# A new order of the opening of an attention and maxout kernel, with some weight work moved to GpSimd

## The chip, the cores and the metric

The kernel runs on one core of a Trainium2 chip. The metric is the device time of one execution in microseconds; 809.75 us is the median of three runs of the kernel before (809.45 to 810.16). Engine names are those of the profile: PE (TensorE matmul), PEld (its weight loads), DVE (VectorE), ACT (ScalarE), POOL (GpSimd), SP (SyncE, which issues the DMAs).

## The reference

There are 4 batches of 12544 tokens with 128 channels, and 32 inducing rows. All is float32.

```
def mab(q, kv):                       # attention without projections
    s = (q @ kv.T) / sqrt(128)
    a = softmax(s, axis=-1)           # maximum taken away, sum + 1e-9
    return a @ kv
h   = mab(inducing, x)                # 32 rows attend over 12544 tokens, per batch
y   = mab(x, h)                       # 12544 tokens attend over the 32 rows
out = maximum(maximum(y @ w1, y @ w2), y @ w3) @ w_out    # 128 -> 768 -> 128
```

The weights come in as 64-bit floats. The kernel reads them as pairs of 32-bit words and makes a float32 out of each pair on the chip.

## The kernel before, in words

**Tiling.** The 98 tiles of 128 tokens of a batch form seven groups: group 0 has 2 tiles, groups 1 to 6 have 16 each. Groups are handled in joint sets (1 with 0, 2 with 3, 4, 5 with 6), which share one running maximum.

**Staging.** The main part is a long run of slots, one per 512 tokens and 128 hidden columns, which is bound by PE: two products of the first layer, a maximum, a split of the result into a high and a low part, three products of the second layer. It needs `us`, the weights already multiplied with `h`. So before the first slot the whole first attention of batch 0 must be done, and the weights be converted. This opening is the head (`head`, L514): a list of steps in text (`HEAD`, L46), each of which issues the instructions of one step. The order of the text is the order on each engine, since every engine runs its own instructions in the order in which they were issued; a step that waits holds up all that stands behind it on its engine. No planner changes the order.

**The steps that the text below speaks of.** After the colon stands the group, the weight (0 is w2, 1 is w_out, 2 is w1, 3 is w3) or the part.

- `T:g.k`, `c:g.k`, `C:g.k`: four transposes of x on PE, and their copy to SBUF by ACT (`c`) or DVE (`C`).
- `S:g` scores (PE), `M:g` maximum (DVE), `D:g` a column of it (ACT), `G:g` and `L:g` the maximum of the joint set (PE, then DVE, L329), `K:g` its copy for the other member (POOL, L348), `E:g` the exponential (ACT, L336), `R:g` a transpose (DVE, L355), `U:g` the weighted sum of x (PE, L370), `H:g` its copy.
- For each weight: `n` the size of the high word (ACT, L187), `r` a scaling of the low word (DVE, L192), `m` a maximum (DVE, L195), `i` a shift (DVE, L199), `v` an integer addition (POOL, L203), `d` the sign put in (DVE, L207), all 128x768. `e:k.part.parts` is the difference of weight k and w2 (DVE, L219).
- `woh` and `wol`: w_out rounded (ACT, L560), and what the rounding left (POOL, L561).
- `least`, `wts`, `maskp`, `lw`, `tot`, `y`, `rec`, `hT`: the seven groups are combined into `h`, divided by the total, and transposed. `maskp` spreads the group weights on POOL (L622); `lw` (L641) sums the totals on DVE.
- `parts` and `p:0.*`, `p:2.*`: scores of the first tokens against `h`, and their softmax in nine steps (mostly DVE, L769 to L793). `turn` transposes the result for PE; `s:0` is the first product of the main part (L848).
- `up:k`, `hi:k`, `lo*:k`: the products of `h` and the weight differences (PE, L671), their high part (ACT, L676), their low part (L686). `mw` multiplies w2 and w_out (PE).

**Loads.** All first loads are issued by SP in one row (`first_loads`, L150, by `LOADS`): x0, w2, x1 in four pieces, x2, x3, w1, x4, x5, w3, x6 in four pieces, w_out. All DMAs share the same engines and come in about in this order.

Of the kernel before, what the change touches and what calls it, by code (L numbers as in the profile page):

```python
# [26 lines left out]
def kernel(ctx, tc, x, xt, ind_t, w1, w2, w3, w_out, out):  # L27
    nc = tc.nc
    B, N, C = x.shape
    M = ind_t.shape[1]  # L30
# [15 lines left out]
    HEAD = """  # L46
        n:0 r:0 F:17 T:1.1 T:1.0 m:0 i:0 C:1.0 c:1.1 T:1.2 c:1.2 T:1.3 C:1.3 T:0.0 S:1 c:0.0 S:0 M:1 M:0 D:1 D:0 v:0
        d:0 T:2.2 C:2.2 T:2.3 c:2.3 T:2.0 c:2.0 G:1 L:1 K:0 T:2.1 C:2.1 E:1 T:3.3 E:0 c:3.3 T:3.2 T:3.0 c:3.0 T:3.1
        n:2 C:3.2 R:1 r:2 m:2 R:0 i:2 c:3.1 S:2 M:2 U:1 S:3 M:3 U:0 HV:1 T:4.1 C:4.1 v:2 D:2 D:3 T:4.2 c:4.2 G:2 L:2
        E:2 d:2 R:2 e:2.0.1 T:4.3 T:4.0 c:4.0 c:4.3 E:3 R:3 T:5.2 c:5.2 n:3 S:4 M:4 D:4 r:3 m:3 i:3 K:3 v:3 U:2  # L50
        T:5.0 c:5.0 T:5.1 c:5.1 G:4 L:4 E:4 T:5.3 C:5.3 T:6.0 C:6.0 T:6.2 c:6.2 T:6.1 c:6.1 R:4 T:6.3 c:6.3 S:5 d:3
        M:5 S:6 M:6 U:3 n:1 m:1 r:1 D:5 D:6 G:5 L:5 K:6 i:1 v:1 H:2 U:4 E:5 e:3.0.2 R:5 E:6 least R:6 H:4 w2T U:5
        U:6 wts lw maskp tot H:5 y:1 y:2 w2h d:1 woh wol y:4 y:5 rec hT parts:0 parts:2 e:3.1.2 p:0.0 p:0.1 p:0.2
        p:0.3 p:2.0 up:0 up:1 hi:0 hi:1 lop:1 p:0.4 p:0.5 p:2.1 p:0.6 p:0.7 up:2 hi:2 mw p:2.2 p:2.3 cw p:0.8 turn:0
        pca:0 turn:1 pca:1 lov:0 lov:2 p:2.4 s:0 up:3 hi:3 N:1 s:1 s:2 p:2.5 N:1 s:3 s:4 p:2.6 N:1 s:5 next p:2.7
        x:0 lov:3 s:6 p:2.8 q:0 q:1 x:1 q:2 q:3 q:4 q:5 q:6 q:7
    """
# [43 lines left out]
    def load_group(b, gi, pieces=1):
        g = groups[gi]
        if g["nt"] == GT:
            xg = xgs_free.pop(0) if xgs_free else xts_free.pop().rearrange("p (t c) -> p t c", c=C)
        else:
            xg = short_x
        n = g["nt"] // pieces
        for k in range(0, g["nt"], n):
            nc.sync.dma_start(out=xg[:, k : k + n, :], in_=xv[b, :, g["t0"] + k : g["t0"] + k + n, :])
# [72 lines left out]

    def weight_size(k):
        v = raws[k].rearrange("p (k two) -> p two k", two=2)
        words[k] = v[:, 0, :], v[:, 1, :]
        sized[k] = hp.tile([P, DF], F32, name="size", tag="size", bufs=2)
        nc.scalar.activation(out=sized[k], in_=words[k][1].bitcast(F32), func=AF.Abs)  # L187

    def weight_rest(k):
        rests[k] = hp.tile([P, DF], F32, name="rest", tag="rest", bufs=2)  # L190
        low = raws[k].rearrange("p (k two) -> p two k", two=2)[:, 0, :]
        nc.vector.tensor_scalar(out=rests[k], in0=low, scalar1=2.0**-51, scalar2=2.0, op0=ALU.mult, op1=ALU.add)  # L192

# [975 lines left out]
```

## Time and profile before

| | us |
|---|---|
| median of three runs | 809.75 |
| span of the profiled execution | 807.8 |
| PE busy, of the span | 799.0 (99%) |
| DVE busy | 647.2 (80%) |
| ACT busy | 714.4 (88%) |
| POOL busy | 656.7 (81%) |

The page gives no time of its own for the profiled execution beside its span. The median stands 1.95 us above the span; that is what lies around it (start and end of the launch). A difference in the span is carried to the median one to one.

A row of the timeline reads: start in us from the span's start, length in us, engine, line, operation, output <- input, partitions x elements, count, and in brackets the idle time before it with what ended it.

### The profile page before, as it was taken

To read this page: it belongs to the slowest core of one execution; us is meant where nothing else is said; L and a number is where in the kernel's file an instruction comes from. 1 tells how busy PE (TensorE), PEld (TensorE's weight loads), DVE (VectorE), ACT (ScalarE), POOL (GpSimd) and SP (SyncE) were. 2 spreads that over 40 slices of the span, in tenths; PEclk is the share of its full clock that TensorE was granted. 3 is DMA by queue.
4 is the path that set the end of the run, shared out by engine and by line. 5 is a ranking of instruction groups with operands and counts; after the bars stand their busy time and mean duration, and the time that the engine had idled before them with its cause. 6 is when DMAs were issued, how large, how long until landed. Compare 5 with 4: busy or idle time off the path is not lost.

```text
span 807.8 us, 15028 instructions
## 1 busy us (share of the span) xinstructions
PE 799.0 (99%) x4565; PEld 629.1 (78%) x4565; DVE 647.2 (80%) x1193; ACT 714.4 (88%) x1435; POOL 656.7 (81%) x637
## 2 busy tenths in 40 slices
PE   8999999999999999999999999999999999999998
PEld 6677778777787787787777877877778778777886
DVE  5988778779787797797976977978878878878874
ACT  4799889889898898898988988989899999999996
POOL 2379888888798898897887988979788879878886
PEclk9999999999999999999999999999999999999999
DMA  8526553442553434435463344334142222222221
GB/s 351 195 101 201 185 170 104 139 140 98 158 178 111 146 121 151 141 108 177 127 184 101 118 155 132 110 125 128 56 110 71 66 78 67 75 77 79 60 80 52
DMA packets 45408, 101.47 MB, mean 126 GB/s; under 512 B 9360, under 2 KB 15376, under 8 KB 40208
## 3 DMA queue, kind: packets, MB, share of 16 engines
q1 hardware_dynamic: 45184, 100.39, 39.8%
q8 instruction: 36, 0.59, 0.3%
q14 instruction: 44, 0.36, 0.1%
q10 hardware_dynamic: 144, 0.13, 0.0%
HBM read 48.12 MB, written 25.69 MB: 91 GB/s over the span
## 4 chain that ended last, share of the span: by engine, by line
PE 95%; DMA 2%; ACT 1%; DVE 0%; issue 0%; SPq 0%; DVEq 0%
PE acc L942 50%; PE pu L848 16%; PE pv L854 16%; PE aux L730 3%; PE acc L936 3%; DMA xg<-in_x_dram 2%; PE acc L488 2%; PE aux L391 2%; PE aux L297 0%; PE acc L370 0%; PE aux L692 0%; ACT ru L863 0%; PE pv L281 0%; PE pu L281 0%; ACT a L336 0%
## 5 line engine op out<-in xcount | busy, mean ns | idle before, releaser
L878 POOL TENSOR_TENSOR lo<-h,hi 128x512 fp32r<-128x512 f32 (+1 forms) x498 | 621.2, 1277 | 111.3 <-ACT hi L870 54.7
L886 DVE TENSOR_TENSOR h<-pv,ru 128x512 f32<-128x512 f32 (+1 forms) x512 | 342.6, 672 | 129.3 <-PE pv L854 104.6
L863 ACT ACTIVATE ru<-pu 128x512 f32<-128x512 f32 (+1 forms) x600 | 368.2, 614 | 66.2 <-PE pu L848 61.9
L870 ACT CAST hi<-h 128x512 fp32r<-128x512 f32 (+1 forms) x512 | 320.1, 625 | 1.1 <-PE acc L942 0.7
L942 PE MATMUL acc<-hi,wo_hi 128*128 128x512 f32 (+1 forms) x601 | 234.8, 391 | 0.0
L848 PE MATMUL pu<-pT,us 128*128 128x512 f32 (+1 forms) x600 | 232.0, 387 | 0.3 <-ACT ru L863 0.2
L854 PE MATMUL pv<-pT,us 128*128 128x512 f32 (+1 forms) x600 | 231.6, 386 | 0.0
L942 PE MATMUL acc<-hi,wo_lo 128*128 128x512 f32 (+1 forms) x601 | 231.4, 385 | 0.0
L942 PE MATMUL acc<-lo,wo_hi 128*128 128x512 f32 (+1 forms) x601 | 231.3, 385 | 0.0
L942 PEld LDWEIGHTS acc<-hi,wo_hi 128*128 128x128 f32 x601 | 112.8, 188 | 41.3 <-issue 19.7
L848 PEld LDWEIGHTS pu<-pT,us 128*128 128x128 f32 x600 | 112.6, 188 | 24.3 <-issue 0.8
L854 PEld LDWEIGHTS pv<-pT,us 128*128 128x128 f32 x600 | 112.6, 188 | 23.5 <-DVE h L886 0.3
L942 PEld LDWEIGHTS acc<-lo,wo_hi 128*128 128x128 f32 x601 | 112.8, 188 | 22.9
L942 PEld LDWEIGHTS acc<-hi,wo_lo 128*128 128x128 f32 x601 | 112.9, 188 | 21.7
L886 DVE TENSOR_TENSOR aux<-pv,ru 128x512 f32<-128x512 f32 x66 | 45.7, 693 | 9.8 <-PE pv L854 3.5
L889 DVE TENSOR_TENSOR lo<-aux,hi 128x512 fp32r<-128x512 f32 x66 | 45.3, 686 | 1.4 <-PE acc L942 0.8
L870 ACT CAST hi<-aux 128x512 fp32r<-128x512 f32 x66 | 41.7, 632 | 0.1
L954 ACT COPY shelf<-acc 128x512 f32<-128x512 f32 (+1 forms) x65 | 39.1, 602 | 0.0
L936 PE MATMUL acc<-pT,us 128*128 128x512 f32 (+1 forms) x100 | 38.8, 388 | 0.0
L432 POOL COPY mq<-mq 32x1 f32<-32x1 f32 (+2 forms) x108 | 20.4, 189 | 5.2
L730 PE MATMUL aux<-xT,hT 128*32 128x512 f32 x184 | 24.5, 605 | 0.0
L488 PEld LDWEIGHTS acc<-xg,aT 128*32 128x32 f32 x576 | 16.8, 110 | 8.5 <-issue 7.8
(186 smaller groups left out, 549.2 us busy)
## 6 DMA issues: line engine op xcount, KB each, us to landing
out_dram<-shelf SPq DMA_DIRECT2D x95, 256.0 KB, 2.0
xg<-in_x_dram SPq DMA_DIRECT2D x22, 1024.0 KB, 5.9
xT<-in_xt_dram SPq DMA_DIRECT2D x18, 1024.0 KB, 5.1
pT<-ph SPq DMA_DIRECT2D x184, 64.0 KB, 2.0
pT<-pl SPq DMA_DIRECT2D x184, 64.0 KB, 2.0
raw<-in_w_dram SPq DMA_DIRECT2D x3, 768.0 KB, 11.0
us<-uh SPq DMA_DIRECT2D x24, 52.0 KB, 3.2
us<-ul SPq DMA_DIRECT2D x24, 52.0 KB, 1.9
```

Of the source, the lines that this page charges most:

```text
L488: nc.tensor.matmul(out=st["h"][q * M : (q + 1) * M, :], lhsT=aT[:, t * M : (t + 1) * M], rhs=row, start=(t < NQ), stop=(t + NQ >= len(rows)),)
L730: nc.tensor.matmul(out=sp[q * M : (q + 1) * M, :w], lhsT=st["hT"][:, :M], rhs=xT[:, q * w : (q + 1) * w], start=True, stop=True)
L848: nc.tensor.matmul(out=pu[:, :w], lhsT=state[c.b]["us"][:, 2 * j * P : (2 * j + 1) * P], rhs=c.pT[:, :w], start=True, stop=True)
L854: nc.tensor.matmul(out=pv[:, : d.w], lhsT=state[d.b]["us"][:, (2 * j + 1) * P : (2 * j + 2) * P], rhs=d.pT[:, : d.w], start=True, stop=True,)
L863: nc.scalar.activation(out=ru[:, :w], in_=pu[:, :w], func=AF.Relu)
L870: nc.scalar.copy(out=hi[:, : c.w], in_=h[:, : c.w])
L878: nc.gpsimd.tensor_sub(**args)
L886: nc.vector.tensor_max(out=h[:, : d.w], in0=pv[:, : d.w], in1=relus.pop(s)[:, : d.w])
L889: nc.vector.tensor_sub(**low)
L936: nc.tensor.matmul(out=c.acc[:, :w], lhsT=us[:, 2 * DF :], rhs=c.pT[:, :w], start=(base == 0), stop=False)
L942: nc.tensor.matmul(out=c.acc[:, cs], lhsT=lhs[:, j, :], rhs=rhs[j][:, cs], start=(j < base and j == 0 and lhs is wo_hi and rhs is c.hh), s ...
L954: (nc.vector.tensor_copy if by_vector else nc.scalar.copy)(out=o[:, : c.w], in_=c.acc[:, : c.w])
```

## The change

It rewrites the list of steps of the head and the order of the loads. Of the loads, the first seven keep their order; after x3 comes w3 in place of w1, and w_out and w1 come last. It adds four kinds of steps that run on GpSimd: `rp` and `mp` (the scaling and the maximum of a weight, in place of DVE), `wohp` (the rounding of w_out, in place of ACT), and `ep` (which the kernel before already knew) is now used for all three differences, in place of DVE. The spreading of the group weights (`maskp`) goes the other way, from POOL to DVE (`mask`). A step `w` is defined and not used.

```diff
-    LOADS = (0, 7, 1, 2, 3, 9, 4, 5, 10, 6, 8)
+    LOADS = """
+        ind x0 w2 x1.0 x1.1 x1.2 x1.3 x2 x3 w3 x4 x5 x6.2 x6.3 x6.0 x6.1 wo w1
+    """
     HEAD = """
-        n:0 r:0 F:17 T:1.1 T:1.0 m:0 i:0 C:1.0 c:1.1 T:1.2 c:1.2 T:1.3 C:1.3 T:0.0 S:1 c:0.0 S:0 M:1 M:0 D:1 D:0 v:0
...
-        M:5 S:6 M:6 U:3 n:1 m:1 r:1 D:5 D:6 G:5 L:5 K:6 i:1 v:1 H:2 U:4 E:5 e:3.0.2 R:5 E:6 least R:6 H:4 w2T U:5
-        U:6 wts lw maskp tot H:5 y:1 y:2 w2h d:1 woh wol y:4 y:5 rec hT parts:0 parts:2 e:3.1.2 p:0.0 p:0.1 p:0.2
-        p:0.3 p:2.0 up:0 up:1 hi:0 hi:1 lop:1 p:0.4 p:0.5 p:2.1 p:0.6 p:0.7 up:2 hi:2 mw p:2.2 p:2.3 cw p:0.8 turn:0
...
+        F:17 T:0.0 c:0.0 T:1.1 C:1.1 T:1.2 T:1.0 C:1.0 T:1.3 c:1.2 C:1.3 S:0 n:0 S:1 M:1
+        M:0 D:1 D:0 T:2.1 T:2.3 C:2.3 mp:0 T:2.2 C:2.2 G:1 T:2.0 c:2.1 L:1 T:3.2 E:1 E:0 T:3.1 C:2.0 R:1 T:3.0 R:0 c:3.2
+        T:3.3 c:3.1 S:2 U:1 n:3 i:0 c:3.0 r:0 C:3.3 S:3 U:0 T:4.2 T:4.3 M:2 T:4.1 rp:3 m:3 M:3 c:4.2 i:3 T:4.0 C:4.3 D:2
+        D:3 G:2 T:5.2 L:2 c:4.1 c:4.0 E:2 E:3 T:5.3 v:0 d:0 T:5.1 K:0 S:4 HV:1 c:5.3 R:3 c:5.1 M:4 c:5.2 D:4 T:5.0 T:6.3
+        T:6.2 c:5.0 G:4 T:6.1 T:6.0 v:3 S:5 d:3 c:6.3 L:4 E:4 ep:3.1.2 C:6.2 C:6.1 c:6.0 R:2 n:1 n:2 R:4 S:6 U:2 rp:1
+        M:5 M:6 D:5 D:6 ep:3.0.2 r:2 m:2 U:3 G:5 L:5 H:2 U:4 i:2 E:5 mp:1 K:3 H:4 K:6 least R:5 i:1 E:6 wts R:6 w2T w2h
+        mask U:5 U:6 H:5 lw y:1 v:2 tot y:2 d:2 y:4 rec v:1 y:5 N:1 hT d:1 parts:0 p:0.0 ep:2.0.1 parts:2 wohp wol p:0.1
+        up:2 up:1 p:0.2 p:2.0 p:0.3 hi:2 p:0.4 p:0.5 up:0 p:0.6 mw p:2.1 hi:1 p:0.7 p:2.2 hi:0 lop:1 p:0.8 lov:0 p:2.3
+        turn:0 lov:2 turn:1 pca:0 p:2.4 cw pca:1 s:0 s:1 s:2 N:1 p:2.5 s:3 s:4 p:2.6 s:5 next x:0 p:2.7 s:6 up:3 q:0 q:1
+        hi:3 p:2.8 x:1 q:2 q:3 lov:3 q:4 N:1 q:5 q:6 q:7
...
+    def weight_rest(k, engine):
+        weight_words(k)
         rests[k] = hp.tile([P, DF], F32, name="rest", tag="rest", bufs=2)
-        low = raws[k].rearrange("p (k two) -> p two k", two=2)[:, 0, :]
-        nc.vector.tensor_scalar(out=rests[k], in0=low, scalar1=2.0**-51, scalar2=2.0, op0=ALU.mult, op1=ALU.add)
-
-    def weight_least(k):
-        nc.vector.tensor_scalar(out=sized[k], in0=sized[k], scalar1=LEAST, scalar2=None, op0=ALU.max)
+        engine.tensor_scalar(out=rests[k], in0=words[k][0], scalar1=2.0**-51, scalar2=2.0, op0=ALU.mult, op1=ALU.add)
+
+    def weight_least(k, engine):
+        engine.tensor_scalar(out=sized[k], in0=sized[k], scalar1=LEAST, scalar2=None, op0=ALU.max)
...
-        nc.sync.dma_start(out=iT, in_=ind_t)
+        first_loads()
         nc.scalar.mul(out=iT, in_=iT, mul=scale)
-        first_loads()
...
-            "r": weight_rest,
-            "m": weight_least,
+            "r": lambda k: weight_rest(k, vec),
+            "rp": lambda k: weight_rest(k, pool),
+            "m": lambda k: weight_least(k, vec),
+            "mp": lambda k: weight_least(k, pool),
...
-            "woh": lambda: nc.scalar.copy(out=wo_hi, in_=wo),
+            "woh": lambda: act.copy(out=wo_hi, in_=wo),
+            "wohp": lambda: pool.tensor_copy(out=wo_hi, in_=wo),
```

In the new list the instructions of DVE from the maximum of group 5 and 6 on are, in order: `L:5 i:2 least R:5 i:1 R:6 mask lw d:2 rec hT d:1 p:0.0`. Those of POOL are, from the first: `mp:0 rp:3 v:0 K:0 v:3 ep:3.1.2 rp:1 ep:3.0.2 mp:1 K:3 K:6 v:2 v:1 ep:2.0.1 wohp wol lop:1`. In the list before, DVE has `L:5 i:1 e:3.0.2 R:5 least R:6 lw d:1 rec hT e:3.1.2 p:0.0`, and POOL `v:0 K:0 v:2 K:3 v:3 K:6 v:1 maskp wol lop:1`.

## Rows read from the trace of the kernel before

**Rows 1.** The page, busy time of PE, and its chain by engine.
```profile
PE 799.0 (99%) x4565; PEld 629.1 (78%) x4565; DVE 647.2 (80%) x1193; ACT 714.4 (88%) x1435; POOL 656.7 (81%) x637
...
PE 95%; DMA 2%; ACT 1%; DVE 0%; issue 0%; SPq 0%; DVEq 0%
```

**Rows 2.** Stretches of the head: start:end, length, each engine's busy time, granted clock, DMA.
```profile
18.00:27.00 9.00, 8.43 (x104) 6.26 (x94) 8.77 (x18) 7.00 (x16) 3.43 (x3) 1.00 1.04 385
27.00:30.00 3.00, 3.00 (x40) 1.49 (x41) 2.79 (x5) 2.71 (x6) 1.06 (x1) 1.00 0.10 33
30.00:34.00 4.00, 3.61 (x94) 2.89 (x87) 4.00 (x10) 2.38 (x9) 2.22 (x2) 1.00 0.00 0
```

**Rows 3.** Timeline of PE: the last transposes, the scores, `up:0` and `s:0`.
```profile
27.34 0.60 PE L281 MATMUL pv<-shelf,xT 128*128 128x128 f32 x4
27.88 1.96 PE L297 MATMUL aux<-xT,shelf 128*32 128x512 f32 x16
...
38.17 1.13 PE L671 MATMUL acc<-shelf,hT 128*128 128x512 f32 x2
...
43.12 0.39 PE L848 MATMUL pu<-pT,us 128*128 128x256 f32 x1
```

**Rows 4.** Issues of the pieces of x6: first and last start, time to landing.
```profile
L109 SPq DMA_DIRECT2D xT<-in_x_dram x4: 328/328/328, 8.6 to 14.2; - x4
...
xT<-in_x_dram SPq DMA_DIRECT2D x1, 256.0 KB, 12.2
```

**Rows 5.** Timeline of POOL in the head.
```profile
14.32 0.18 POOL L348 COPY mneg<-mneg 128x1 f32<-128x1 f32 x1 [4.12 <-DVE mneg L329]
18.63 1.82 POOL L203 TENSOR_TENSOR rest<-rest,size 128x768 int32<-128x768 int32 x1 [4.13 <-DVE size L199]
20.78 0.85 POOL L348 COPY mneg<-mneg 128x1 f32<-128x1 f32 x1 [0.33 <-DVE mneg L329]
...
31.67 0.45 POOL L348 COPY mneg<-mneg 128x1 f32<-128x1 f32 x1 [3.61 <-DVE mneg L329]
32.22 2.02 POOL L203 TENSOR_TENSOR rest<-rest,size 128x768 int32<-128x768 int32 x1
...
37.16 1.90 POOL L561 TENSOR_TENSOR wo_lo<-xT,wo_hi 128x768 fp32r<-128x768 f32 x1 [2.40 <-ACT wo_hi L560]
```

**Rows 6.** Timeline of DVE in the head.
```profile
20.64 0.95 DVE L207 SCALAR_TENSOR_TENSOR dst<-raw,rest 128x768 uint32<-128x768 uint32 x1
...
22.26 0.92 DVE L219 TENSOR_TENSOR shelf<-dst,xT 128x768 f32<-128x768 f32 x1
...
29.91 0.69 DVE L307 TENSOR_REDUCE mq<-aux 128x1 f32<-128x512 f32 x1 [0.21 <-PE aux L297]
...
31.45 0.16 DVE L329 TENSOR_REDUCE mneg<-acc 128x1 f32<-128x8 f32 x1
31.53 0.55 DVE L199 TENSOR_SCALAR size<-size 128x768 uint32<-128x768 uint32 x1
...
32.46 0.70 DVE L355 STREAM_TRANSPOSE aT<-a 128x512 f32<-128x512 f32 x1
...
33.13 0.71 DVE L355 STREAM_TRANSPOSE aT<-a 128x512 f32<-128x512 f32 x1
33.76 0.50 DVE L641 TENSOR_TENSOR lw<-w,lst 128x7 f32<-128x7 f32 x1
34.30 0.16 DVE L643 TENSOR_REDUCE l<-lw 128x1 f32<-128x7 f32 x1
...
36.16 0.35 DVE L652 RECIPROCAL rec<-rec 128x32 f32<-128x32 f32 x1 [0.26 <-DVE rec L651]
36.62 0.29 DVE L657 TENSOR_TENSOR hT<-pu,rec 128x128 f32<-128x128 f32 x1
...
37.73 0.40 DVE L769 STREAM_TRANSPOSE pv<-pv 128x192 f32<-128x192 f32 x1 [0.35 <-PE pv L748]
```

**Rows 7.** POOL by groups, first two us: operations with one input or none; busy us, mean ns.
```profile
masks.py:199 POOL TENSOR_SCALAR_AFFINE_SELECT shelf<-shelf 128x128 f32<-128x128 f32 x1 | 0.3, 295 | 0.1
```

More of the change, by code (lines that the diff above doesn't have):

```diff
@@ L46 @@
     HEAD = """
-        n:0 r:0 F:17 T:1.1 T:1.0 m:0 i:0 C:1.0 c:1.1 T:1.2 c:1.2 T:1.3 C:1.3 T:0.0 S:1 c:0.0 S:0 M:1 M:0 D:1 D:0 v:0
[L48 to L51, printed above, removed]
-        M:5 S:6 M:6 U:3 n:1 m:1 r:1 D:5 D:6 G:5 L:5 K:6 i:1 v:1 H:2 U:4 E:5 e:3.0.2 R:5 E:6 least R:6 H:4 w2T U:5
-        U:6 wts lw maskp tot H:5 y:1 y:2 w2h d:1 woh wol y:4 y:5 rec hT parts:0 parts:2 e:3.1.2 p:0.0 p:0.1 p:0.2
-        p:0.3 p:2.0 up:0 up:1 hi:0 hi:1 lop:1 p:0.4 p:0.5 p:2.1 p:0.6 p:0.7 up:2 hi:2 mw p:2.2 p:2.3 cw p:0.8 turn:0
-        pca:0 turn:1 pca:1 lov:0 lov:2 p:2.4 s:0 up:3 hi:3 N:1 s:1 s:2 p:2.5 N:1 s:3 s:4 p:2.6 N:1 s:5 next p:2.7
-        x:0 lov:3 s:6 p:2.8 q:0 q:1 x:1 q:2 q:3 q:4 q:5 q:6 q:7
+        F:17 T:0.0 c:0.0 T:1.1 C:1.1 T:1.2 T:1.0 C:1.0 T:1.3 c:1.2 C:1.3 S:0 n:0 S:1 M:1
[8 more added lines that the diff above has]
+        hi:3 p:2.8 x:1 q:2 q:3 lov:3 q:4 N:1 q:5 q:6 q:7
     """
@@ L98, with space_for, load_tiles, load_group @@
     xv = x.rearrange("b (p t) c -> b p t c", t=NT)
[L101 to L109, printed above, removed]
+    def space_for(gi):
+        if groups[gi]["nt"] < GT:
+            return short_x
+        return xgs_free.pop(0) if xgs_free else xts_free.pop().rearrange("p (t c) -> p t c", c=C)
+    def load_tiles(b, gi, xg, a, z):
+        t0 = groups[gi]["t0"]
+        nc.sync.dma_start(out=xg[:, a:z, :], in_=xv[b, :, t0 + a : t0 + z, :])
+    def load_group(b, gi):
+        xg = space_for(gi)
+        load_tiles(b, gi, xg, 0, groups[gi]["nt"])
         return xg
@@ L144, in load_raw @@
         return r
-    srcs = [w2.bitcast(U32), w_out.bitcast(U32).rearrange("(j p) c -> p j c", p=P), w1.bitcast(U32), w3.bitcast(U32)]
+    srcs = {
+        "w2": (0, w2.bitcast(U32)),
+        "wo": (1, w_out.bitcast(U32).rearrange("(j p) c -> p j c", p=P)),
+        "w1": (2, w1.bitcast(U32)),
+        "w3": (3, w3.bitcast(U32)),
+    }
     raws = {}
-    FULLS = [gi for gi in LOADS if 0 < gi < NG]
+    SPARE_HOME = NG - 1
     def first_loads():
-        for what in LOADS:
-            if what < NG:
-                state[0]["xg"][what] = load_group(0, what, pieces=4 if what in (FULLS[0], FULLS[-1]) else 1)
-            else:
-                raws[what - NG] = load_raw(srcs[what - NG])
+        xgs = state[0]["xg"]
+        xgs.update({gi: space_for(gi) for gi in range(NG)})
+        for what in LOADS.split():
+            if what == "ind":
+                nc.sync.dma_start(out=iT, in_=ind_t)
+            elif what in srcs:
+                k, src = srcs[what]
+                raws[k] = load_raw(src)
+            else:
+                gi, piece = ([int(n) for n in what[1:].split(".")] + [None])[:2]
+                a, z = (0, groups[gi]["nt"]) if piece is None else (4 * piece, 4 * piece + 4)
+                load_tiles(0, gi, xgs[gi], a, z)
     ident = place(P)
@@ L181, with weight_words, weight_size @@
     words, sized, rests, floats = {}, {}, {}, {}
-    def weight_size(k):
+    def weight_words(k):
         v = raws[k].rearrange("p (k two) -> p two k", two=2)
         words[k] = v[:, 0, :], v[:, 1, :]
+    def weight_size(k):
+        weight_words(k)
         sized[k] = hp.tile([P, DF], F32, name="size", tag="size", bufs=2)
         nc.scalar.activation(out=sized[k], in_=words[k][1].bitcast(F32), func=AF.Abs)
-    def weight_rest(k):
+    def weight_rest(k, engine):
+        weight_words(k)
         rests[k] = hp.tile([P, DF], F32, name="rest", tag="rest", bufs=2)
-        low = raws[k].rearrange("p (k two) -> p two k", two=2)[:, 0, :]
-        nc.vector.tensor_scalar(out=rests[k], in0=low, scalar1=2.0**-51, scalar2=2.0, op0=ALU.mult, op1=ALU.add)
-    def weight_least(k):
-        nc.vector.tensor_scalar(out=sized[k], in0=sized[k], scalar1=LEAST, scalar2=None, op0=ALU.max)
+        engine.tensor_scalar(out=rests[k], in0=words[k][0], scalar1=2.0**-51, scalar2=2.0, op0=ALU.mult, op1=ALU.add)
+    def weight_least(k, engine):
+        engine.tensor_scalar(out=sized[k], in0=sized[k], scalar1=LEAST, scalar2=None, op0=ALU.max)
     def weight_shift(k):
@@ L199, in weight_shift, with weight_join @@
         nc.vector.tensor_scalar(out=bits, in0=bits, scalar1=3, scalar2=None, op0=ALU.logical_shift_left)
+    def weight_join(k):
+        whole = rests[k].bitcast(I32)
+        nc.gpsimd.scalar_tensor_tensor(
+            out=whole, in0=sized[k].bitcast(I32), scalar=8, in1=whole, op0=ALU.mult, op1=ALU.add
+        )
     def weight_whole(k):
@@ L360, in attend_sums @@
         st = state[b]
-        xg, aT = st["xg"].pop(gi), st["a"].pop(gi)
+        xg, aT = st["xg"][gi], st["a"].pop(gi)
         members = JOINT[LEADER[gi]]
-        if gi == FULLS[-1]:
+        if gi == SPARE_HOME:
             xts_free.append(xg.rearrange("p t c -> p (t c)"))
@@ L554, in head @@
             "n": weight_size,
-            "r": weight_rest,
-            "m": weight_least,
+            "r": lambda k: weight_rest(k, vec),
+            "rp": lambda k: weight_rest(k, pool),
+            "m": lambda k: weight_least(k, vec),
+            "mp": lambda k: weight_least(k, pool),
             "i": weight_shift,
+            "w": weight_join,
             "v": weight_whole,
             "d": weight_sign,
-            "woh": lambda: nc.scalar.copy(out=wo_hi, in_=wo),
+            "woh": lambda: act.copy(out=wo_hi, in_=wo),
+            "wohp": lambda: pool.tensor_copy(out=wo_hi, in_=wo),
             "wol": lambda: nc.gpsimd.tensor_sub(out=wo_lo, in0=wo, in1=wo_hi.bitcast(F32)),
@@ L665, in first_products @@
     def first_products(st, which, bank):
-        if which == 0:
+        if "us" not in st:
             st["us"] = bp.tile([P, UW], F32R, name="us", tag="us")
```

## The prediction

> **What bounds the kernel now.** I read the page first: PE is busy 99% of the span, and the chain of work that ended last lies on PE for 95% [rows 1]. Behind the head there is nothing to win for a change that touches the head alone; it moves the time by as much as it moves the first product of the main part, `s:0`, at 43.12 [rows 3]. The dense part then ends as much earlier or later. So the question is which wait ends last before `s:0`. For that I read, in this order, the stretches of the head, then the timelines of PE, POOL and DVE side by side.
>
> In the stretches the reader is to see that loads aren't the limit at the end. DMA works to the 27th us; the last piece of x6 was issued at 14.2 and landed 12.2 later, at 26.4 [rows 4], but its transposes came at 27.34 behind the ones before them, on a PE that was busy for 3.00 of 3 us [rows 2, 3]. Before that PE stood idle for 9.00 − 8.43 = 0.57 us in 18 to 27 [rows 2]. From 30 on DVE is the full engine (4.00 of 4) [rows 2], and the chain runs through it: `L:5` (31.45), the transposes `R:5` and `R:6`, the reciprocal, `hT` (36.62), then the softmax `p:0.0` (37.73), and from there 43.12 − 37.73 = 5.39 us to `s:0` [rows 3, 6].
>
> In POOL's rows the reader is to see one more thing. A copy of 128x1 took 0.18 us at 14.32, but 0.85 at 20.78, which ends at 21.63, just when DVE's sign step `d` (20.64 + 0.95 = 21.59) is done; and 0.45 at 31.67, ending at 32.12, when DVE's shift of 31.53 (+ 0.55 = 32.08) is done. The other way round, `lw`, seven columns, took 0.50 on DVE from 33.76, and ended at 34.26, with POOL's `v` (32.22 + 2.02 = 34.24) [rows 5, 6]. So POOL and DVE shut each other out, for a whole instruction, where DVE works from SBUF on two inputs (`d`, `lw`) or on one at double rate (the shift: 0.55 for 768 columns, against 0.92 for the two-input difference of 768 [rows 6]). Operations of DVE that read PSUM, and the transposes, ran beside `v` at their usual length: `R:5` 0.70 and `R:6` 0.71, both inside `v` [rows 5, 6].
>
> By the Trainium skill, SBUF — State Buffer, section "SBUF: two separate sides", the two engines share one pair of ports as an exclusive lock, held for the whole instruction, against DVE operations in a two-port mode or with two SBUF inputs; the trace agrees, with the 0.85, the 0.45 and the 0.50. What the trace of before does not show is the one case of a double-rate DVE operation that waits for POOL; by the page it would, and then the second case below falls away.
>
> **The change, part by part.**
>
> *Loads.* x6 comes about 2 us earlier, w1 takes w_out's place as the last. PE can win at most the 0.57 us that it stood idle; w1's conversion `n:2, r:2, m:2` simply stands where w_out's `n:1, r:1, m:1` stood. SP issues as many loads as before, in one row, and the later ones of batch 1 are not needed before the main part. I take 0 to −0.6.
>
> *Work taken from DVE.* Up to `L:5` it is four scalings and maxima and the difference of w1, 4 x 0.55 + 0.92 = 3.1 us. It does not come off the path there: `M:6` waited 0.21 for PE [rows 6], not for DVE. So 0.6, PE's idle time, is about the most by which `L:5` can come earlier.
>
> *Work given to POOL.* A one-input operation of 128x768 is not in the trace. From below, 128x128 took 0.295 and 128x1 0.18 [rows 5, 7], so 0.18 + 768/128 x 0.115 = 0.87; from above, a two-input one took 1.82 to 1.90 [rows 5]. I take 1.0, near the one-input row. It is not its length that I count, but whom it shuts out: `i:0`, `m:3`, `d:0` and `r:2` on DVE now fall due while POOL works on `rp:3`, `v:0`, `v:3` or the row `ep:3.1.2 rp:1 ep:3.0.2 mp:1`. A part of one instruction each, 0 to 1 us, partly in the shadow of other waits; I set it against the 0.6 and take `L:5` at 31.45 as before. Bounds: 30.85 without such waits, and 34.1 if the new operations take 1.9 (1.9 for the one in front of `r:2`, 0.8 more of `mp:1` in front of `v:2`).
>
> By the Trainium skill, GPSIMD Engine Reference, section "4.1 Engine selection", an operation with one input runs there at about line rate; with the 1.2 GHz of its section "1. Specifications" that is an estimate of 768/1.2 = 640 ns, which no row here shows; the sum would by it come to some 0.3 less.
>
> *The end of the head.* Here three POOL instructions of 1.8 to 1.9 us (`v:2`, `v:1`, `ep:2.0.1`) stand just where DVE has five two-input or double-rate ones (`i:1`, `mask`, `lw`, `d:2`, `d:1`), in front of the chain. From `L:5` at 31.45:
>
> - `i:2` 31.53 to 32.08, as the shift did before [rows 6]; `v:2` on POOL 32.13 to 33.95 (1.82 [rows 5]).
> - `R:5` 32.46 to 33.16, as before. `i:1` is due at 33.1 and waits for `v:2`, 0.85: 33.95 to 34.50. `R:6` stands behind it: 34.45 to 35.16, where it ended at 33.84 before (+1.3).
> - `v:1` needs `i:1`: 34.55 to 36.37. `mask` is due at 35.16 and waits 1.2 for `v:1`. Its length is between 0.29 (128x128) and 0.92 (128x768) [rows 6]; 0.38 in proportion: to 36.75. The group sums `y` and U:6 are in its shadow.
> - `lw` and its sum, 0.16 each (34.30 [rows 6]), to 37.1; `d:2` 0.95 to 38.05; `rec` is the reciprocal with the idle time in front of it, 0.35 + 0.26, and an addition as short as the 0.16 of 34.30, 0.8 in all: to 38.85, `hT` 0.3 to 39.2. It was 36.91 before: +2.3.
> - `ep:2.0.1` needs `d:2`: POOL 38.1 to 40.0 (1.90 as `wol`). `d:1`, new between `hT` and `p:0.0`, is due at 39.2, waits 0.8, and ends at 40.95. `p:0.0` then starts at 40.95, and not at 37.73: **+3.2**.
>
> Behind that the nine softmax steps are the same: 5.39 us to `s:0`. The `up` products can start when `ep` is done, at 40.0, and three of 1.13 at most (38.17 [rows 3]) end at 43.4, and `mw` behind them well before `s:0` is due at 46.3. `wohp` and `wol` on POOL (1.0 + 1.9 behind `d:1`, to 43.9) are done before `s:0`, and `wo_lo` is used behind it; ACT, through which the chain doesn't pass here, loses the rounding. Cost 0.
>
> Sum: 0 + 3.2 + 0; 807.8 becomes 811.0, and with the 1.95 us around the span, 809.75 becomes **812.9**. The bounds of this case: 812.3 with `L:5` at 30.85, 815.6 with it at 34.1.
>
> **The rivals.**
>
> 1. *Only two-input operations of DVE wait for POOL.* For it: `lw` is the only DVE instruction whose wait for POOL is seen whole. Against it: the copy of 0.45 behind the shift. `i:1` then doesn't wait (`v:1` starts at 33.95, ends 0.57 earlier), and `L:5` comes 0.6 earlier: 3.2 − 1.2 = +2.0, **811.7**.
> 2. *The engines don't get in each other's way here* (POOL's int32 and one-input operations leave room for DVE). Not slower: `hT` comes 0.2 earlier than before, since `R:6`, `mask` and `lw` follow at once; `d:1` (0.95) then fills the place of the half difference and of the 0.35 that `p:0.0` waited. **809.5**. Against it: the 0.50 of `lw`, behind this same `v`. It decides if `mask` starts within 0.1 of the end of `R:6`.
> 3. *DVE's queue sets the pace of the whole head* (8.77 of 9 us and 4.00 of 4 [rows 2]), and what is taken from it shows: of the 3.1 us, some 2, since not all of it falls due after 18 us. **807.7**. Against it: `M:6` waits for PE.
> 4. *The granted clock falls in the pauses of PE* that the waits make. It is 1.00 (2.4 GHz) in every stretch [rows 2]; at 1.2 GHz the three `up` products on the path behind `hT`, some 3 us, take 3 us more on top of the forecast: **816**. No row of before shows a fall.
>
> **How the numbers follow.** Forecast 55%, rival 1 15%, rival 2 15%, rival 3 10%, rival 4 5%. About 0.2%, 1.6 us, is what a measurement of this kernel can tell from no change. Slower by more: all of the forecast, most of rival 1 (0.09, its price being near the limit) and rival 4, 0.69; the same: 0.06 and 0.13 of rival 2, 0.19; faster: rival 3 and the rest of rival 2, 0.12. The range runs from 809.0 to 815.0; it leaves out rivals 3 and 4 and the far end of the forecast. The likeliest case's own range is 812.0 to 815.6.
>
> **What would show it.** `i:1` (128x768 shift on DVE) that ends with `v:2`, and lasts longer than 0.55 or starts late; `mask` that ends just behind `v:1`; `d:1` that ends about 0.95 behind `ep:2.0.1`; `hT` near 39 and `p:0.0` near 41, `s:0` near 46.3, and the same 5.4 us between them; `L:5` near 31.5; POOL's new operations near 1 us. I am wrong if `p:0.0` comes before 39, if `mask` runs inside `v:1`, or if `s:0` is late and the end is not.

## The result and the profile after

The changed kernel is slower: 814.16 us (median of 5 runs, 813.55 to 815.25) against 809.75 (5 runs beside it, 809.45 to 810.29). The ratio is 1.0055, with a 95% interval of 1.0042 to 1.0067. The same kernel in a second series gave 814.05, ratio 1.0056 (1.0043 to 1.0069). The forecast was 812.9, the range 809.0 to 815.0.

The profiled execution is the slowest of its five, with an own time of 815.25 and a span of 813.5; the other four have spans of 811.7 to 812.9. The page (engine: busy, share, instructions; TensorE's clock in slices of 20 us; the chain by engine):

```profile
PE 802.2 (99%) x4565; PEld 629.9 (77%) x4565; DVE 649.9 (80%) x1189; ACT 711.7 (87%) x1432; POOL 666.6 (82%) x644
...
PEclk9989999999999999999999999999999999999999
...
PE 95%; DMA 2%; DVE 1%; ACT 1%; issue 0%; SPq 0%; DVEq 0%; ACTq 0%
```

As before [rows 1], PE is busy 99% of the span and the chain lies on it. What is new on the page is the 8 in the third slice of PEclk: the granted clock was lower somewhere between 41 and 61 us; the stretches below show that the fall began at 39. The stretches of the head (columns as in [rows 2]: length, then PE, PEld, DVE, ACT, POOL, then the clock):

```profile
27.00:30.00 3.00, 3.00 (x62) 1.67 (x64) 1.23 (x3) 2.68 (x5) 3.00 (x4) 1.00 0.10 33
30.00:34.00 4.00, 2.48 (x66) 1.99 (x59) 3.83 (x9) 1.79 (x7) 2.40 (x4) 1.00 0.00 0
34.00:38.00 4.00, 2.64 (x69) 1.89 (x67) 4.00 (x5) 1.89 (x7) 3.21 (x2) 1.00 0.01 4
...
39.00:45.00 6.00, 5.99 (x33) 2.87 (x33) 5.65 (x14) 0.90 (x2) 4.44 (x3) 0.50 0.67 240
```

Two things stand in them. From 27 to 30 DVE does only 1.23 us of work, where it did 2.79 [rows 2]: it waits. And from 39 to 45 the clock is 0.50 (1.2 GHz of 2.4), after eight microseconds, 30 to 38, in which PE was busy 5.1 of 8. DVE's timeline (columns as in [rows 6]; line numbers have moved: L381 is `R`, L333 `M`, L355 `L`, L219 `i`, L233 `d`, L798 `p:0.0`) shows where the time went:

```profile
18.67 1.21 DVE L215 TENSOR_SCALAR size<-size 128x768 f32<-128x768 f32 x1
...
30.00 0.71 DVE L381 STREAM_TRANSPOSE aT<-a 128x512 f32<-128x512 f32 x1 [1.77 <-ACT size L207]
30.64 1.25 DVE L333 TENSOR_REDUCE mq<-aux 128x1 f32<-128x512 f32 x2
...
32.74 0.16 DVE L355 TENSOR_REDUCE mneg<-acc 128x1 f32<-128x8 f32 x1
32.85 0.56 DVE L219 TENSOR_SCALAR size<-size 128x768 uint32<-128x768 uint32 x1
...
34.38 1.44 DVE L219 TENSOR_SCALAR size<-size 128x768 uint32<-128x768 uint32 x1
35.74 0.70 DVE L381 STREAM_TRANSPOSE aT<-a 128x512 f32<-128x512 f32 x1
36.37 1.66 DVE L651 TENSOR_TENSOR mask<-shelf,w 128x224 f32<-128x224 f32 x1
37.95 0.15 DVE L670 TENSOR_TENSOR lw<-w,lst 128x7 f32<-128x7 f32 x1
...
39.79 0.29 DVE L686 TENSOR_TENSOR hT<-pu,rec 128x128 f32<-128x128 f32 x1
40.00 1.86 DVE L233 SCALAR_TENSOR_TENSOR xT<-raw,rest 128x768 uint32<-128x768 uint32 x1
41.78 0.39 DVE L798 STREAM_TRANSPOSE pv<-pv 128x192 f32<-128x192 f32 x1
```

and POOL's, beside it, whom these DVE instructions waited for (L215 is `mp`, L212 `rp`, L229 `v`, L245 `ep`, L589 `wohp`; in DVE's rows L215 is `m`, L212 `r`, L651 `mask`):

```profile
17.63 1.83 POOL L229 TENSOR_TENSOR rest<-rest,size 128x768 int32<-128x768 int32 x1 [0.96 <-DVE rest L212]
...
27.31 0.95 POOL L212 TENSOR_SCALAR rest<-raw 128x768 f32<-128x768 uint32 x1
...
29.19 2.14 POOL L215 TENSOR_SCALAR size<-size 128x768 f32<-128x768 f32 x1
...
33.57 1.84 POOL L229 TENSOR_TENSOR rest<-rest,size 128x768 int32<-128x768 int32 x1
35.96 1.81 POOL L229 TENSOR_TENSOR rest<-rest,size 128x768 int32<-128x768 int32 x1 [0.56 <-DVE size L219]
39.24 1.81 POOL L245 TENSOR_TENSOR shelf<-dst,xT 128x768 f32<-128x768 f32 x1 [1.46 <-DVE dst L233]
41.93 0.83 POOL L589 CAST wo_hi<-xT 128x768 fp32r<-128x768 f32 x1 [0.88 <-DVE xT L233]
```

PE's timeline, the last scores of the head and the sums `U:2` and `U:3` behind them, the first `up` product (L700), and `s:0` (L877), which answer to [rows 3]:

```profile
27.08 1.93 PE L323 MATMUL aux<-xT,shelf 128*32 128x512 f32 x16
28.82 1.93 PE L396 MATMUL acc<-xg,aT 128*32 128x128 f32 x64
...
42.22 2.07 PE L700 MATMUL pv<-shelf,hT 128*128 128x512 f32 x2
...
48.79 0.38 PE L877 MATMUL pu<-pT,us 128*128 128x256 f32 x1 [0.18 <-ACT pT L558]
```

Cut as the prediction cut it, against the rows of before [rows 3, 6]:

| | before | after | difference | forecast |
|---|---|---|---|---|
| to `L:5` | 31.45 | 32.74 | +1.29 | 0 |
| `L:5` to `p:0.0` | 6.28 | 9.04 | +2.76 | +3.2 |
| `p:0.0` to `s:0` | 5.39 | 7.01 | +1.62 | 0 |
| `s:0` | 43.12 | 48.79 | +5.67 | +3.2 |
| span | 807.8 | 813.5 | +5.7 | +3.2 |

So the span did move with `s:0`, one to one. The middle term came near the forecast; the first and the last were put at nothing and were not. The experiments were to say what made each of the three.

### The profile page after: what moved, and what is told of

The parts are those of the page before. It is cut to its first block, busy times and chain, and to the rows that moved or that the text cites. A ratio compares the mean times of both kernels' runs of the same rounds, so it can differ in the third digit from the quotient of the medians.

```text
span 813.5 us, 14942 instructions
## 1 busy us (share of the span) xinstructions
PE 802.2 (99%) x4565; PEld 629.9 (77%) x4565; DVE 649.9 (80%) x1189; ACT 711.7 (87%) x1432; POOL 666.6 (82%) x644
## 4 chain that ended last, share of the span: by engine, by line
PE 95%; DMA 2%; DVE 1%; ACT 1%; issue 0%; SPq 0%; DVEq 0%; ACTq 0%
PE acc L971 50%; PE pu L877 17%; PE pv L883 17%; PE aux L759 3%; PE acc L965 3%; DMA xg<-in_x_dram 2%; PE acc L514 2%; PE aux L417 2%; PE aux L323 0%; PE aux L721 0%; PE pv L700 0%; PE pv L307 0%; PE pu L307 0%; PE aux L700 0%; DVE mask L651 0%
## 5 line engine op out<-in xcount | busy, mean ns | idle before, releaser
L877 PE MATMUL pu<-pT,us 128*128 128x512 f32 (+1 forms) x600 | 232.0, 387 | 0.5 <-ACT pT L560 0.3
L877 PEld LDWEIGHTS pu<-pT,us 128*128 128x128 f32 x600 | 112.6, 188 | 24.6 <-ACT hi L899 0.8
```

The source lines that it names most:

```text
L877: nc.tensor.matmul(out=pu[:, :w], lhsT=state[c.b]["us"][:, 2 * j * P : (2 * j + 1) * P], rhs=c.pT[:, :w], start=True, stop=True)
```

## The experiments

Each run's times stand against those of the kernel before in the same series, 809.62, 809.74 or 809.65 us. Diffs of the list of steps show the places that differ.

**The same kernel again.** No edit.

> The changed kernel once more, for its spread and a second profile. My theory has three parts for the +5.7 us of its profiled span: L:5 comes 1.3 us later (32.74 for 31.45) because R:4 waits for a buffer; L:5 to p:0.0 takes 2.75 us more (9.04 for 6.28), the waits of VectorE for GpSimd; p:0.0 to s:0 takes 1.6 us more (7.01 for 5.39), the granted clock at half from 39 to 45.8. If the last part is the clock, the time goes with the length of that stretch: 813.5 to 815.3, and the first two parts repeat within 0.2. Rival: the third part is the new order of ACT's steps, then it repeats at 1.6 whatever the clock does.

814.05 us (813.78 to 815.55). `L:5` stands at 32.69 and `p:0.0` at 41.74, within 0.05 of the first profile; `p:0.0` to `s:0` took 5.59, not 7.01. The first two terms belong to the kernel. The third goes with the clock, which in this execution was back at 1.00 from 44 on (the stretches, columns as above):

```profile
40.00:42.00 2.00, 1.95 (x24) 0.81 (x24) 2.00 (x2) 0.00 (x0) 1.12 (x2) 0.50 0.85 360
42.00:44.00 2.00, 2.00 (x8) 0.98 (x5) 1.86 (x7) 0.65 (x2) 1.92 (x2) 0.77 0.46 74
```

**PE's pauses filled.** `F:n` is n matmuls whose result nobody reads.

```diff
-        r:2 m:2 U:3 G:5 L:5
+        r:2 m:2 U:3 F:6 G:5 L:5
...
-        mask U:5 U:6 H:5
+        mask U:5 F:4 U:6 F:4 H:5
```

> The changed kernel with 14 more unread products on TensorE (6 behind U:3, 4 behind U:5, 4 behind U:6) in its pauses between 31 and 38 us; nothing else differs. Theory (the clock takes the third part): granted clock 1.00 in every stretch of the head, p:0.0 to s:0 5.4 to 5.8 us, time 812.2 to 812.9. Rival (the order of ACT's steps takes it): 814.2 within 0.4, p:0.0 to s:0 stays near 7.

813.87 us (813.65 to 814.5); ratio 1.0051 (1.0037 to 1.0065). The stretches show PE busy 3.72 and 3.88 of 4 us (2.48 and 2.64 in after), and a clock of 1.00 throughout:

```profile
30.00:34.00 4.00, 3.72 (x75) 2.99 (x67) 3.75 (x9) 1.71 (x7) 2.44 (x4) 1.00 0.00 0
34.00:38.00 4.00, 3.88 (x76) 3.02 (x74) 4.00 (x4) 1.96 (x7) 3.30 (x2) 1.00 0.02 4
...
40.00:42.00 2.00, 1.81 (x26) 0.95 (x27) 2.00 (x3) 0.00 (x0) 1.15 (x1) 1.00 0.90 381
```

PE's timeline of the same run, the first `up` product and `s:0`:

```profile
41.30 1.13 PE L700 MATMUL pv<-shelf,hT 128*128 128x512 f32 x2
...
47.18 0.39 PE L877 MATMUL pu<-pT,us 128*128 128x256 f32 x1 [0.17 <-ACT pT L558]
```

The first product took its 1.13 again, and `p:0.0` (41.89) to `s:0` took 5.29, close to the forecast's 5.39. The third term is the clock. The median, though, fell by 0.2 only, outside what I expected and inside the rival's band; the rival's other sign, `p:0.0` to `s:0` near 7, did not come. By the medians and by the repeat (5.59 − 5.29) a usual execution of the changed kernel loses 0.2 to 0.3 to the clock, and the one first profiled lost 1.7; I had taken that one for the rule.

**`R:4` later.** DVE waited 1.77 us in front of `R:4`, and `M:5` and `M:6` stood behind it.

```diff
-        R:4 S:6 U:2 rp:1 M:5 M:6 D:5 D:6
+        S:6 U:2 rp:1 M:5 M:6 R:4 D:5 D:6
```

> The changed kernel with the step R:4 moved behind M:6, so that the two maxima on VectorE don't stand behind R:4's wait for U:2. Theory: M:5 and M:6 end near 29.7 and not at 31.9; L:5 comes at 31.5 to 32.0 (not before w1 has landed and n:2 and m:2 are done, near 30.5), 0.8 to 1.2 us earlier, and the time is 813.0 to 813.4. Rival (r:2 and m:2 behind GpSimd's row set L:5, not R:4): L:5 stays near 32.7 and the time at 814.2.

813.82 us (813.7 to 814.11); ratio 1.0049 (1.0036 to 1.0062). DVE's timeline:

```profile
29.48 0.69 DVE L333 TENSOR_REDUCE mq<-aux 128x1 f32<-128x512 f32 x1 [0.23 <-PE aux L323]
...
30.92 1.15 DVE L212 TENSOR_SCALAR rest<-raw 128x768 f32<-128x768 uint32 x1
...
32.45 0.15 DVE L355 TENSOR_REDUCE mneg<-acc 128x1 f32<-128x8 f32 x1
```

and on POOL's, the instruction that came to light:

```profile
29.51 2.14 POOL L215 TENSOR_SCALAR size<-size 128x768 f32<-128x768 f32 x1
```

`M:6` came at 29.48, which is 0.43 earlier than in the kernel before [rows 6]: so the new list does bring the scores forward, and `R:4`'s wait had hidden it. What of this is due to the loads no run separates; in the new list `U:2` also stands behind `S:6`, where it stood in front of the last transposes. But `L:5` gained only 0.3, since `r:2`, a double-rate operation, now waited for `mp:1`, whose 2.14 us had lain in the shadow of `R:4`'s wait. So it takes more than `R:4`'s wait to hold `L:5` where it was; the rival was right in the main. The span tells less here: `s:0` came at 46.79, 0.54 before that of the repeat, but the span, 812.3, is no shorter than the repeat's 812.0. In this profiled execution the clock stayed at 1.00 up to 48 and fell behind `s:0`, to 0.53 in 48 to 50. PE had been busy 5.7 of 8 us from 30 to 38.

**`i:1` in front of `i:2`.** The maximum that it needs is named earlier in the list, at the same place among GpSimd's steps, so that `i:1` no longer falls into `v:2`.

```diff
-        ep:3.0.2 r:2 m:2 U:3 G:5 L:5 H:2 U:4 i:2 E:5 mp:1 K:3 H:4 K:6 least R:5 i:1 E:6
+        ep:3.0.2 mp:1 r:2 m:2 U:3 G:5 L:5 H:2 U:4 i:1 i:2 E:5 K:3 H:4 K:6 least R:5 E:6
```

> The changed kernel with VectorE's shift i:1 in front of i:2 (and mp:1 issued earlier in the text, at the same place among GpSimd's steps), so that no step of GpSimd runs when i:1 is due. Theory (a double-rate operation of VectorE with one input waits for GpSimd as a two-input one does): i:1 takes 0.55 and not 1.44, R:6 ends near 35.0 and not 36.4, mask still waits for one v, but ends near 36.2 and not 38.0; hT near 38 and time 812.2 to 812.8. Rival (i:1's 1.44 is not GpSimd's doing): nothing moves by more than 0.4.

813.98 us (813.44 to 815.18); ratio 1.0052 (1.0039 to 1.0064). DVE's timeline:

```profile
33.00 1.02 DVE L219 TENSOR_SCALAR size<-size 128x768 uint32<-128x768 uint32 x2
...
35.54 0.71 DVE L651 TENSOR_TENSOR mask<-shelf,w 128x224 f32<-128x224 f32 x1
36.17 1.77 DVE L670 TENSOR_TENSOR lw<-w,lst 128x7 f32<-128x7 f32 x1
```

and beside it on POOL's the two additions, `v:2` and `v:1`, in one row:

```profile
34.17 3.75 POOL L229 TENSOR_TENSOR rest<-rest,size 128x768 int32<-128x768 int32 x2 [0.58 <-DVE mmin L642]
```

The two shifts together took 1.02, where `i:1` alone had taken 1.44: its length was POOL's doing, not its own. Yet `hT` came only 0.2 earlier (39.59). `mask` now slipped in between the two additions (36.25 is its end, and 36.0 that of `v:2`), and `lw`, seven columns, waited for the second one: 1.77 us. The wait had moved one instruction on.

**`v:1` behind `hT` as well.** On top of the last: `v:1` goes behind `ep:2.0.1`, and `d:1`, `wohp` and `wol`, which need it, into the softmax steps.

```diff
-        rec v:1 y:5 N:1 hT d:1 parts:0 p:0.0 ep:2.0.1 parts:2 wohp wol p:0.1
+        rec y:5 N:1 hT parts:0 p:0.0 ep:2.0.1 v:1 parts:2 p:0.1
...
-        p:0.4 p:0.5 up:0
+        p:0.4 d:1 p:0.5 wohp wol up:0
```

> The changed kernel with i:1 in front of i:2 as in i1_first, and now also v:1 behind ep:2.0.1 on GpSimd and d:1, wohp, wol behind p:0.4, so that of w_out's steps none stands between R:6 and p:0.0. Theory (in i1_first the exclusion only went on to lw, which waited 1.77 us for v:1): mask and lw wait for v:2 alone, lw ends near 36.5 and not at 38, hT near 38.3, p:0.0 near 39.4 and not 41.7; time 812.0 to 812.8. Rival (the wait moves on once more, to d:2 or ep:2.0.1 for the up products): p:0.0 earlier, s:0 not, 813.6 to 814.2.

812.64 us (811.86 to 813.05); ratio 1.0033 (1.0021 to 1.0046), as expected. DVE's timeline:

```profile
35.44 0.71 DVE L651 TENSOR_TENSOR mask<-shelf,w 128x224 f32<-128x224 f32 x1
36.07 0.15 DVE L670 TENSOR_TENSOR lw<-w,lst 128x7 f32<-128x7 f32 x1
...
39.01 0.40 DVE L798 STREAM_TRANSPOSE pv<-pv 128x192 f32<-128x192 f32 x1 [0.73 <-PE pv L777]
...
40.97 0.96 DVE L233 SCALAR_TENSOR_TENSOR xT<-raw,rest 128x768 uint32<-128x768 uint32 x1
```

With no addition of POOL in front of `hT` but `v:2`, `lw` takes 0.15, and `hT` (37.99) comes 1.8 us earlier than in after. `p:0.0` gains 1.0 more, 2.8 in all, since `d:1` no longer stands between the two; but `d:1` comes back at 40.97, among the softmax steps, and `p:0.0` to `s:0` (45.10) takes 6.09 for 5.29. This is why the time gains less than `p:0.0` does.

**The five moves alone.** The order and the loads of before, with `mp:0`, `mp:1`, `rp:3`, `rp:1`, `wohp`.

```diff
-        n:0 r:0 F:17 T:1.1 T:1.0 m:0 i:0
+        n:0 r:0 F:17 T:1.1 T:1.0 mp:0 i:0
...
-        r:3 m:3 i:3
+        rp:3 m:3 i:3
...
-        n:1 m:1 r:1 D:5
+        n:1 mp:1 rp:1 D:5
...
-        d:1 woh wol
+        d:1 wohp wol
```

> The kernel before, with its own order of steps and loads, and only the five moves of the change's name: m of w2 and w_out and r of w3 and w_out on GpSimd, the rounding of w_out on GpSimd. Theory (GpSimd's longer operations stand in the chain and shut VectorE out; the maximum takes 2.13 us there, the scaling 0.93): slower, s:0 2 to 3 us later than 43.12, time 811.5 to 812.7. Rival (relief of VectorE helps or does nothing): 808.5 to 810.

811.05 us (11 runs, 810.86 to 811.28); ratio 1.0016 (1.0008 to 1.0025). Slower, by less than I had put it at. DVE's timeline:

```profile
32.01 1.30 DVE L219 TENSOR_SCALAR size<-size 128x768 uint32<-128x768 uint32 x1 [0.28 <-POOL size L215]
```

and POOL's:

```profile
29.85 2.13 POOL L215 TENSOR_SCALAR size<-size 128x768 f32<-128x768 f32 x1 [1.68 <-ACT size L207]
31.94 0.94 POOL L212 TENSOR_SCALAR rest<-raw 128x768 f32<-128x768 uint32 x1
```

`i:1` waits 0.28 for the maximum, and then lasts 1.30, since `rp:1` begins just ahead of it.

**The moves undone in the new order.** The five edits above the other way round, in the changed kernel.

> The changed kernel with those five moves taken back (on VectorE and ScalarE again), its new order, its new loads, the differences on GpSimd and mask on VectorE kept. Theory (the order is made for the moves, and the waits at its end, i:1, mask, d:1 against v:2, v:1, ep, stay): no gain, 814.0 to 815.5. Rival (the five moves are the loss): 810 to 812.

815.14 us (814.58 to 815.3); ratio 1.0064 (1.0052 to 1.0077). The new order alone (with the loads, `ep` and `mask`) costs 5.4 us; the moves give some of it back, 1.0 by the medians (815.14 to 814.16), though the intervals of the two ratios overlap. In the traces `L:5` is at 33.67 without the moves and at 32.74 with them; without them DVE does the scaling of w_out in front of `L:5`, and its maximum in front of `i:1`. Here DVE's timeline names another releaser for `R:4` (L396 is `U`):

```profile
30.47 0.71 DVE L381 STREAM_TRANSPOSE aT<-a 128x512 f32<-128x512 f32 x1 [1.77 <-PE acc L396]
```

That is `U:2`, which reads the buffer that `R:4` writes; in the profile of after `U:2` and the ACT instruction that was named ended together. In both, `R:4` starts 1.18 us behind `U:2` (30.00 for 28.82, and 30.47 for 29.29), while the ACT instruction ends 0.08 and 0.24 before it; what `R:4` reads was written by 27.3 in after. The kernel gives these transposes two buffers.

**Maxima alone, and scalings with the rounding alone,** in the order of before: the two halves of the five moves.

> The order and the loads of before, with two of its steps alone on GpSimd: the maxima of w2 and w_out (m:0, m:1). Both scalings (r:3, r:1) stay on DVE and the rounding (woh) on ACT. With all five moved, the maximum of w_out ran 29.85 to 31.98 on POOL, the scaling rp:1 31.94 to 32.88 directly behind it, and the shift i:1, which needs the maximum, began on DVE at 32.01 and ended at 33.31 (1.30 instead of 0.55): p:0.0 38.87, median 811.05. My theory: the two only cost together. The maximum alone makes i:1 0.5 us late (it begins at 32.0, where it began at 31.53), but with nothing behind it on POOL i:1 has its 0.55: p:0.0 about 38.2, median 810.1 to 810.6. Rival: the 2.13 us of the maximum is the whole price, wherever rp:1 stands: i:1 ends at 33.3 again, p:0.0 at 38.8, median 810.9 to 811.2.

> The order and the loads of before, with three of its steps alone on GpSimd: the scalings of w3 and w_out (r:3, r:1) and the rounding of w_out (woh). Both maxima stay on DVE. My theory: the scaling of w_out, 0.94 us, then begins as soon as v:3 is done on POOL (28.2) and is over near 29.2, so it shuts nothing out that is on the path; L:5 31.4 to 31.6, i:1 0.55, p:0.0 37.6 to 38.0, median 809.5 to 810.0. Rival: a scaling costs as a maximum does, by the DVE instruction that it shuts out: d:3 and the maximum m:1 on DVE wait for it, L:5 comes at 32 or later, median 810.5 or more.

Maxima: 810.14 us (11 runs), ratio 1.0006 (0.9998 to 1.0015). Scalings and rounding: 809.84 (11 runs), ratio 1.0001 (0.9992 to 1.001). Neither differs from before by more than can be measured (809.65 in this series); in the two traces `p:0.0` comes at 38.16 and 37.87, where it was 37.73 [rows 6]. DVE's timeline with the maxima alone:

```profile
32.04 0.56 DVE L219 TENSOR_SCALAR size<-size 128x768 uint32<-128x768 uint32 x1 [0.23 <-POOL size L215]
```

`i:1` is as late as with all five moves, but not stretched. The price of the five, 1.3 us, is thus no sum of their lengths: about 0.5 for the late maximum, 0.2 for the scalings and the rounding, and 0.6 for the scaling that the maximum pushes in front of `i:1`. As neither half alone is clear of the noise, this division leans on `p:0.0` in the traces: 0.43, 0.14, and with all five 1.14.

**All repairs together.** `v:1` late as above, `R:4` behind `M:6`, and the maximum of w_out back on DVE behind `M:6`.

```diff
-        R:4 S:6 U:2 rp:1 M:5 M:6 D:5 D:6 ep:3.0.2 mp:1 r:2 m:2
+        S:6 U:2 rp:1 M:5 M:6 m:1 R:4 D:5 D:6 ep:3.0.2 r:2 m:2
```

> v1_late with R:4 behind M:6 (as in r4_late) and m of w_out back on VectorE, behind M:6, so that GpSimd's maximum of 2.13 us doesn't stand in front of r:2 and m:2. Theory (the parts add up): L:5 near 31.7 and not 32.7, p:0.0 near 38.4, s:0 near 44.5, time 810.9 to 811.7, still above before, since w1's conversion stands last in the chain. Rival (another wait takes the place of mp:1's): as v1_late within 0.4.

811.11 us (11 runs, 810.64 to 811.83); ratio 1.0016 (1.0007 to 1.0025). DVE's timeline:

```profile
31.61 0.16 DVE L355 TENSOR_REDUCE mneg<-acc 128x1 f32<-128x8 f32 x1
...
37.81 0.40 DVE L798 STREAM_TRANSPOSE pv<-pv 128x192 f32<-128x192 f32 x1 [0.74 <-PE pv L777]
...
39.76 0.96 DVE L233 SCALAR_TENSOR_TENSOR xT<-raw,rest 128x768 uint32<-128x768 uint32 x1
```

PE's row of `s:0`, and the stretch behind it:

```profile
43.88 0.38 PE L877 MATMUL pu<-pT,us 128*128 128x256 f32 x1 [0.18 <-ACT pT L558]
...
46.00:50.00 4.00, 3.91 (x17) 3.54 (x17) 3.02 (x8) 3.79 (x12) 2.83 (x5) 0.57 0.02 4
```

`L:5` and `p:0.0` are back within 0.2 us of before; `s:0`, at 43.88, is not (43.12). Between the two stands `d:1`, 0.96, for which this list leaves no place in front of `hT`, because `d:2` is there. In the kernel before `d:2` was long done, at 20.64 [rows 6]. That w1, loaded last, is what is left of the loss at `s:0`, 0.76, is read from these rows; a list with w1 early and all else as here was not run. In the profiled execution more was lost behind `s:0`: from there to the end it took 766.0 us, and 764.7 in before and after, with a clock of 0.57 in 46 to 50. So three causes, the buffer wait, POOL's additions beside DVE's short operations (with `d:1` in front of `p:0.0`), and the length of the maximum, make up 3.0 of the 4.4 us; of the 1.4 left, no run tells `d:1`'s part from the clock's.

## Why the prediction was right, and where not

**The chain from `L:5` to `p:0.0` (+3.2): right, instruction by instruction.** Counted from `L:5`, `i:1` ends at 3.08 (forecast 3.05), `R:6` at 3.70 (3.71), `mask` at 5.29 (5.30), and `p:0.0` starts at 9.04 (9.50). The three waits are there: `i:1` 1.44 instead of 0.55, `d:1` 1.86 instead of 0.95, and `mask` 1.66, ending 0.26 behind `v:1` (0.25 behind `v:2` in the runs where it took 0.71, so that no run shows its own length). The 0.46 too much are spread from `lw` on; the largest piece, some 0.2, is `rec`, which took 0.63 up to the start of `hT` and not the 0.8 that I had put together for it.

**Rival 1, that only two-input operations wait: wrong.** `i:1` has one input, at double rate, and waited; moved away from `v:2` it took 0.5. So the page of the Trainium skill that I cited, SBUF — State Buffer, section "SBUF: two separate sides", holds in its second half too: the lock also shuts out DVE's two-port modes, if the double rate that the rows show is one of them. `m:3` (1.21 at 18.67, beside an addition that ends at 19.46) and `r:2` (1.15 in the run with `R:4` late) agree.

**`L:5` stays at 31.45: wrong, by 1.29.** The step had it right that PE can win some 0.6 (`M:6` 0.43 earlier once nothing stood in front), but not what eats it. I looked for DVE waits behind POOL alone. I did not follow the buffers: `R:4` now stands in front of `M:5`, and writes where `U:2` still has to read, behind `S:6` on PE. In this order all of the 1.29 is there, `M:6` ending at 31.89 for 30.60. Behind it stood the term of my upper bound, 1.9 for a POOL operation in front of `r:2`: with `R:4` out of the way it came out at 2.14, and `L:5` gained only 0.3. The bound of 34.1 held by luck, for it was not set for a buffer.

**A one-input operation of 1.0 us on POOL (bounds 0.87 to 1.9): right for two kinds, wrong for the third.** The scaling took 0.91 to 0.95, the rounding 0.83, just under the lower bound; the maximum took 2.13, longer than the two-input addition (1.82). The Trainium skill (GPSIMD Engine Reference, section "4.1 Engine selection") lets one-input operations run at about line rate, 640 ns by my estimate; none of the three did, by the maximum it is off more than threefold, and the measurement decides. In the changed kernel this cost little by itself, as it lay behind `R:4`.

**`p:0.0` to `s:0` unchanged: right at full clock (5.29), short of what was measured.** Rival 4's mechanism, with 5% and 3 us, did occur: PE's pauses, 5.1 busy of 8 us, were followed by the lower clock. I treated it as an alternative to the forecast, though it follows from it: a forecast that stalls PE by 3 us must price the clock as a part of itself. It cost 0.2 to 0.3 us in a usual execution, by the medians and the repeat, and 1.7 in the one first profiled.

**The time around the span.** I carried 1.95 us; the runs show 1.7 to 1.9 for either kernel, which is 0.2 of the forecast at most.

Added up for the repeat: 1.24 + 2.77 + 0.20 = 4.2, which is the difference of its span from before (812.0 − 807.8); by the medians, 814.16 − 809.75, it is 4.4. The forecast was 1.3 short. `R:4`'s wait put 1.3 on top of it and the clock 0.2 to 0.3, and the middle term, 0.4 below the forecast, took some of that back: that the time lies within the range is partly luck, since two errors went opposite ways.

## What to carry to other kernels

When an order written by hand is changed, follow three things for every instruction that now stands earlier: its inputs, the other engine that it can shut out or be shut out by, and the last reader of the buffer that it writes; the third is the one that no timeline of before shows. Work given to GpSimd is priced not by its own length alone but by the short VectorE instructions that it shuts out, and taking one of them out of the way only helps if the next one behind it isn't shut out instead. A wait of an in-order engine hides the causes behind it, so a cause taken away alone shows less than it is worth: `R:4` moved alone brought `L:5` forward by 0.3 us, and by 1.2 (32.82 to 31.61) together with the maximum; the maximum alone was not tried in the new order. Nor must the end move with the first product: in two profiles the clock fell behind `s:0`, and took back there a part or all of what the head had won.

## What was not expected of the hardware

- On GpSimd, over 128x768 elements, a maximum with an immediate operand took 2.12 to 2.15 us, a multiplication with addition 0.91 to 0.95, a rounding copy 0.83.
- A short VectorE operation can pass between two GpSimd instructions that follow each other, and the next one not: `mask`, due while `v:2` ran, passed in 0.71, and `lw` behind it waited 1.77 for `v:1`.
- The length of a fall of the clock differs between executions of one program: 0.50 over all of 39 to 45 in one, back to 1.00 before 44 in the other. In the profiled executions of the repaired kernel and of the one with `R:4` later a fall came behind `s:0`, in 46 to 50 (0.57) and from 48 (0.53 to 50), and from `s:0` to the end they took 1.3 and 0.8 us longer; without the moves one came already in 34 to 38 (0.57). What sets its place wasn't settled.
